# Top-k attention and a SwiGLU block on one core: the first nine units handled straight through, FFN block 0 by halves, rounding steps set between single top-k operations, and a new order of exponentials, sums and normalization within a unit

## The chip, the core and the metric

The kernel runs on one core of one Trainium2 chip. The core has five engines, each with its own instruction queue, worked through in order: TensorE (PE; its weight loads are shown apart as PEld), VectorE (DVE), ScalarE (ACT), GpSimd (POOL) and SyncE (SP), which here issues all transfers between HBM and the on-chip memory SBUF. Matmul results land in PSUM, a second on-chip memory, from which ScalarE copies them. The metric is the device time in microseconds (us).

## What is computed

```python
# q, k, v: (8, 8, 576, 64) float32; the three weights are float64
scores = scale * np.matmul(q, k.transpose(0, 1, 3, 2))
kth = np.partition(scores, -32, axis=-1)[..., -32:-31]
scores = np.where(scores >= kth, scores, -1e9)
attn = np.exp(scores - scores.max(-1, keepdims=True))
attn = attn / (attn.sum(-1, keepdims=True) + 1e-09)
o = np.matmul(attn, v)
x = o.transpose(0, 2, 1, 3).reshape(4608, 512)
g = x @ w_gate                                   # (512, 1536)
out = (g * (1 / (1 + np.exp(-g))) * (x @ w_val)) @ w_out   # (1536, 512)
```

Only the 32 largest of the 576 scores of each query count. The attention output of all heads is one token matrix `x`, on which the gated feed-forward block (FFN) works.

## The kernel before

**Units.** Attention is cut into 160 units, in the order batch (8), query tile (5), head pair (4): `units`, line 219. Four query tiles have 128 queries, so a unit holds two heads of 128 x 576 scores; the fifth has 64 queries, and its unit holds both heads on 128 partitions at once, half the work ("half units", units 16 to 19 of each batch of 20).

**A unit's steps.** `prep` (once per head pair and batch) transposes k and q on TensorE and ScalarE copies them to `kqT`. `scores` makes four PSUM banks `s`, which ScalarE copies to `sc`. `select` finds the 32 largest on VectorE: per head four MAX8 with three MATCH_REPLACE8 between them, and then one operation that sets `e` to a large negative number where a score is below the 32nd. `penalize` adds `sc` to `e` on POOL. `weigh` takes the exponential on ScalarE, with the row sum `tot`. `normalize` adds 1e-9 and takes the reciprocal of `tot` on VectorE, then ScalarE multiplies `e` by it. `turn` transposes `e` on TensorE, nine 128 x 128 tiles through three PSUM tiles `etps` (of four, one and four), and ScalarE copies them to `et`. `values` multiplies with v into `av`, and ScalarE copies that to the token block `xT`.

**PSUM.** The tiles `kqps`, `s`, `etps` and `av` share one pool of five buffers, given out in turn; `f` and `o_ps` of the FFN share three.

**FFN.** 4608 tokens make 18 blocks of 256. `feed` gives out a block in 36 pieces: 24 of four matmuls `f` (half a product of gate or value), then 12 of two matmuls `o_ps`. When a product is complete, a closure for ScalarE is put on `on_act` (gate: tanh, scale, add one; value: a copy), and one for POOL's multiplication on `on_pool`; `flush` records them. A block can start when its 256 tokens are there for all four head pairs (line 482). Pieces are paid with `credit`: 4.6 per pass of the loop (2.3 for a half unit), at most 8 saved.

**Rounding.** The weights are float64. `rounded` (line 92) turns a piece of 128 x 256 into fp32 from its two 32-bit halves, `low` and `high`: a transfer `w`, two operations on POOL, two on ScalarE and three on VectorE, 72 pieces in all. `weights` runs the pieces as a pipeline: one `rounding` step records the transfer of piece n, the first operations of piece n-3, the bit operations of n-4 and the last of n-5. `need` runs further steps when the FFN reaches a weight that isn't ready.

**The order.** The program text is the order: lines 576 to 590 chain the instructions of each compute engine in the order in which they are recorded. Pass n of the main loop (line 523) records, in this order: the penalty of unit n-1, the normalization of n-2, the values of n-3, the scores of n+1, and then the eleven or so steps of the top-k of n, with rounding steps, FFN pieces, the transposes of n-2 and the exponentials of n-1 between them. The VectorE part of `normalize(n-1)` stands between top-k steps.

## Time and profile before

| | |
|---|---|
| median of 3 runs | 1973.16 us (1972.95 to 1974.05) |
| the profiled execution | 1975.04 us, of which the span of its instructions is 1973.2 us |
| TensorE busy | 1779.5 us, 90% of the span |
| VectorE busy | 1640.1 us, 83% |
| ScalarE busy | 1156.0 us, 59% |
| POOL busy | 773.0 us, 39% |
| mean granted TensorE clock | 0.942 of full speed |

In a wait line, "A <- B: t, n, l" says that engine and line A stood idle until B for t us in all, n times, at most l us. In a timeline line the columns are start (us), duration (us), engine, line, operation, output<-inputs, shape, and the number of instructions taken together. One matmul of the program is two records in the trace, except for transposes, which are one. A line number with L is a line of the kernel. Matmul ends are modelled, so the next start is the better measure.

### The profile page before, as it was taken

The page shows a single profiled execution, that of the slowest core. Times are in us where ns is not written, and L with a number is a line of the kernel's source. Part 1 is how long each engine was busy: PE and PEld are TensorE (multiplying, and loading weights), DVE is VectorE, ACT ScalarE, POOL GpSimd, SP SyncE. Part 2 cuts the span into 40 slices and gives each one's busy share as a digit, 9 for nine tenths or more (in the row PEclk, how much of TensorE's full clock was granted, in tenths as well). Part 3 has the DMA queues.
Part 4 walks back from the last instruction along what each step waited for, and adds up shares of the span by engine and source line. Part 5 has one row for each costly group of instructions (what it writes and reads, how often), then busy time and mean ns, then how long its engine had stood idle before and what let it go on. Part 6 is the DMA issues. An engine that isn't in the chain of part 4 may idle for free.

```text
span 1973.2 us, 29487 instructions
## 1 busy us (share of the span) xinstructions
PE 1779.5 (90%) x10144; PEld 1297.7 (66%) x10144; DVE 1640.1 (83%) x3708; ACT 1156.0 (59%) x2821; POOL 773.0 (39%) x686
## 2 busy tenths in 40 slices
PE   3444779989999999999999999989999999899899
PEld 1223655847686867686768686858686867586666
DVE  5999687998889998989799898998898988889700
ACT  3555455656575656666667566656675656565512
POOL 2555453424334434343434352434343434243412
PEclk6566789999999999999999999999999999999999
DMA  5222111100030002100030002000120002000000
GB/s 153 84 80 75 43 50 43 44 12 1 9 79 11 1 12 57 30 1 11 4 78 7 12 2 68 18 11 1 33 54 11 1 14 50 11 1 11 1 11 11
DMA packets 111253, 59.58 MB, mean 30 GB/s; under 512 B 89088, under 2 KB 97280, under 8 KB 111104
## 3 DMA queue, kind: packets, MB, share of 16 engines
q1 hardware_dynamic: 111104, 57.70, 11.1%
q8 instruction: 80, 1.31, 0.3%
q14 instruction: 69, 0.57, 0.1%
HBM read 48.23 MB, written 9.44 MB: 29 GB/s over the span
## 4 chain that ended last, share of the span: by engine, by line
PE 78%; DVE 13%; issue 3%; ACT 3%; POOL 2%; SPq 1%; DMA 1%; POOLq 0%; ACTq 0%; DVEq 0%
PE f L418 37%; PE o_ps L452 18%; PE av L364 7%; PE etps L335 6%; PE s L256 6%; DVE m L277 5%; DVE rest L281 4%; PE s L242 2%; PE av L355 1%; PE kqps L211 1%; DVE bits L117 1%; DVE e L287 1%; DVE bits L114 1%; ACT e L308 1%; POOL bits L121 1%
## 5 line engine op out<-in xcount | busy, mean ns | idle before, releaser
L299 POOL TENSOR_TENSOR e<-e,sc 128x1152 f32<-128x1152 f32 (+1 forms) x160 | 383.0, 2394 | 731.3 <-DVE e L287 487.1
L277 DVE MAX8 m<-rest 128x8 f32<-128x576 f32 x864 | 613.7, 747 | 2.2
L418 PE MATMUL f<-xT,wg 128*128 128x256 f32 x1728 | 423.1, 391 | 16.7 <-ACT xT L379 16.7
L281 DVE MATCH_REPLACE8 rest<-m,rest 128x576 f32<-128x576 f32 x576 | 423.9, 743 | 0.0
L418 PE MATMUL f<-xT,wv 128*128 128x256 f32 x1728 | 409.3, 384 | 0.0
L452 PE MATMUL o_ps<-wo,h 128*128 128x512 f32 x864 | 400.1, 599 | 4.4 <-DVE wo L124 4.4
L418 PEld LDWEIGHTS f<-xT,wg 128*128 128x128 f32 x1728 | 323.4, 194 | 89.7 <-issue 27.8
L336 ACT COPY et<-etps 128x512 f32<-128x512 f32 (+1 forms) x448 | 195.1, 477 | 305.8 <-PE etps L335 305.2
L418 PEld LDWEIGHTS f<-xT,wv 128*128 128x128 f32 x1728 | 321.0, 193 | 48.3 <-issue 9.9
L335 PE MATMUL etps<-ident,e 128*128 128x128 f32 (+1 forms) x1312 | 207.4, 289 | 122.2 <-ACT sc L261 70.5
L335 PEld LDWEIGHTS etps<-ident,e 128*128 128x128 f32 (+1 forms) x1312 | 168.0, 148 | 202.8 <-issue 99.1
L323 ACT ACTIVATE e<-e,tot 128x576 f32<-128x576 f32 x288 | 209.5, 770 | 133.7 <-DVE tot L320 133.7
L452 PEld LDWEIGHTS o_ps<-wo,h 128*128 128x128 f32 x864 | 153.6, 190 | 163.6 <-issue 156.0
L439 POOL TENSOR_TENSOR h<-h,half_g 128x512 f32<-128x512 f32 x108 | 137.9, 1277 | 265.3 <-ACT h L438 258.8
L308 ACT ACTIVATE e<-e,bias 128x576 f32<-128x576 f32 x288 | 221.6, 776 | 4.1 <-POOL e L299 4.1
L277 DVE MAX8 m<-sc 128x8 f32<-128x576 f32 x288 | 205.1, 749 | 10.1 <-ACT sc L261 10.1
L281 DVE MATCH_REPLACE8 rest<-m,sc 128x576 f32<-128x576 f32 x288 | 212.0, 743 | 0.0
L256 PE MATMUL s<-kqT 64*128 64x288 f32 x1024 | 172.7, 459 | 11.4 <-ACT kqT L216 11.3
L364 PE MATMUL av<-et,v 128*64 128x128 f32 (+1 forms) x2560 | 178.5, 281 | 2.1 <-ACT et L336 1.0
L261 ACT COPY sc<-s 128x288 f32<-128x288 f32 x512 | 167.2, 416 | 12.8 <-PE s L256 12.3
L318 DVE TENSOR_SCALAR tot<-tot 128x2 f32<-128x2 f32 (+1 forms) x160 | 25.4, 159 | 168.0 <-ACT e L308 168.0
L444 POOL TENSOR_TENSOR h<-h,val 128x512 f32<-128x512 f32 x108 | 139.1, 1288 | 60.7 <-ACT val L443 60.3
(45 smaller groups left out, 1459.8 us busy)
## 6 DMA issues: line engine op xcount, KB each, us to landing
kq_in<-in_k_dram SPq DMA_DIRECT2D x64, 128.0 KB, 2.8
kq_in<-in_q_dram SPq DMA_DIRECT2D x64, 128.0 KB, 3.0
v<-in_v_dram SPq DMA_DIRECT2D x32, 256.0 KB, 3.0
w<-in_moe_w_gate_dram SPq DMA_DIRECT2D x24, 256.0 KB, 2.7
w<-in_moe_w_val_dram SPq DMA_DIRECT2D x24, 256.0 KB, 2.7
w<-in_moe_w_out_dram SPq DMA_DIRECT2D x24, 256.0 KB, 2.5
out_dram<-o SPq DMA_DIRECT2D x40, 128.0 KB, 2.4
out_dram<-o SPq DMA_DIRECT2D x16, 256.0 KB, 2.4
```

Source lines behind the costliest of these rows:

```text
L256: nc.tensor.matmul(ps[:, 0:half], slab[d, q0 : q0 + P], slab[d, k0 : k0 + half])
L261: nc.scalar.copy(sc[:, i * half : (i + 1) * half], ps[:, 0:half])
L277: nc.vector.max(m[:, t, 8 * r : 8 * r + 8], cur[:, hs])
L281: nc.vector.match_replace(rest[:, hs], m[:, t, 8 * r : 8 * r + 8], cur[:, hs], LOWEST)
L299: nc.gpsimd.tensor_tensor(e[:, every], e[:, every], sc[:, every], ALU.add)
L308: nc.scalar.activation(e[:, hs], e[:, hs], AF.Exp, bias=bias[:, t : t + 1], scale=scale, accum_out=tot[:, t : t + 1],)
L323: nc.scalar.mul(e[:, hs], e[:, hs], tot[:, t : t + 1])
L335: nc.tensor.transpose(ps[0:kl, c * P : (c + 1) * P], e[:, k0 : k0 + kl], ident[:])
L336: nc.scalar.copy(et[0:kl, c0 : c0 + cn, :], ps[0:kl, 0 : cn * P].rearrange("p (c j) -> p c j", c=cn),)
L364: nc.tensor.matmul(av[hh * R : (hh + 1) * R, 0:ql], v_last[:, hh, :] if c == J else vt[:, hh, c, :], moving, start=last and c == 0, stop=c ...
L418: nc.tensor.matmul(ps[:, i, :], w[:, c, m * P : (m + 1) * P], x[:, c, :], start=(c == 0), stop=(c == KC - 1),)
L452: nc.tensor.matmul(ps[:], hs[m // 2][:, m % 2, t * P : (t + 1) * P], wo[:, m, :], start=(m == 0), stop=(m == MC - 1),)
```

## The change

- **Rounding.** The absolute value is taken first (ScalarE), then clamped from below and above on POOL, then shifted; the sign and top bit now come from `high` itself. One VectorE operation of three is gone. Small values are no longer set to zero but clamped to the smallest size. `w` has 7 buffers instead of 4, `bits` 3, and the pipeline's last lag is 6 instead of 5.
- **Rounding steps** are no longer recorded in bunches but by a rate, 10/15 per top-k operation up to pass 4 and 6/15 after it. `select` yields after every single operation.
- **Head.** In passes 0 to 8 unit n-1 goes through all its steps (exponentials, sums, normalization, transposes, values) in pass n. q, k and v of the first batch's later pairs are loaded from within the passes.
- **Block 0** of the FFN runs in two halves of 128 tokens; the first can begin after unit 3 instead of unit 7. A head pass earns 8 credits; at most 10 are saved.
- **Order in a unit, in all passes.** ScalarE's FFN work is flushed and the exponentials of unit n-1 recorded right after the first FFN piece, ahead of the copies of the scores of n+1. After the head, the sum's VectorE operations stand at the end of the top-k.
- `sc` has 2 buffers instead of 3, `m` 2 instead of 3. At m = 6 of an output tile, pending ScalarE and POOL work is flushed.

```diff
@@ rounded @@
-        w = ffn.tile([P, n, 2], I32, tag="w", name="w", bufs=4)
+        w = ffn.tile([P, n, 2], I32, tag="w", name="w", bufs=7)
...
-        nc.gpsimd.tensor_scalar(
-            hi[:], high.bitcast(FP32), HUGE, -HUGE, ALU.min, ALU.max
-        )
+        size = conv.tile([P, n], FP32, tag="size", name="size")
+        nc.scalar.activation(size[:], high.bitcast(FP32), AF.Abs)
+        nc.gpsimd.tensor_scalar(size[:], size[:], HUGE, LEAST, ALU.min, ALU.max)
         ulps = conv.tile([P, n], I32, tag="ulps", name="ulps")
         nc.scalar.mul(ulps[:], low.bitcast(U32), 2.0**-29)
-        size = conv.tile([P, n], FP32, tag="size", name="size")
-        nc.scalar.activation(size[:], hi[:], AF.Abs)
         yield
...
         nc.vector.tensor_scalar(
-            bits[:], hi, 3, 0x3FFFFFFF, ALU.logical_shift_left, ALU.bitwise_and
-        )
-        nc.vector.scalar_tensor_tensor(
-            out=bits[:], in0=hi, scalar=-0x40000000, in1=bits[:],
-            op0=ALU.bitwise_and, op1=ALU.bitwise_or,
+            bits[:], size[:].bitcast(I32), 3, 0x3FFFFFFF,
+            ALU.logical_shift_left, ALU.bitwise_and,
         )
         nc.gpsimd.tensor_tensor(bits[:], bits[:], ulps[:], ALU.add)
         yield
         nc.vector.scalar_tensor_tensor(
-            out=dst, in0=size[:], scalar=LEAST, in1=bits[:].bitcast(FP32),
-            op0=ALU.is_ge, op1=ALU.mult,
+            out=dst.bitcast(I32), in0=high, scalar=-0x40000000, in1=bits[:],
+            op0=ALU.bitwise_and, op1=ALU.bitwise_or,
         )
@@ weights @@
-            for lag in (5, 4, 3, 0):
+        lags = (6, 4, 3, 0)
@@ scores, select @@
-        sc = work.tile([P, 2 * S], FP32, tag="sc", name="sc", bufs=3)
+        sc = work.tile([P, 2 * S], FP32, tag="sc", name="sc", bufs=2)
-        m = small.tile([P, 2, TOP_K], FP32, tag="m", name="m")
+        m = small.tile([P, 2, TOP_K], FP32, tag="m", name="m", bufs=2)
@@ feed @@
+        halves = [slice(0, P), slice(P, BLK)] if kb == 0 else [slice(0, BLK)]
+        for c in halves:
+            while done[kb] < NHP * c.stop:
+                yield 0
...
                 need(8 * MS + 2 * m + 2)
+                if m == 6:
+                    flush(on_act)
+                    flush(on_pool)
@@ before the loop @@
     load(0)
-    rounding(3)
+    rounding(4)
     load(1)
-    for i in range(NHP):
-        if i > 1:
-            load(i)
-        load_v(i)
@@ the loop @@
+    HEAD = 2 * NHP + 1
+    due = [0.0]
     for n in range(NU + 3):
+        head = n < HEAD
...
+        turned = turn(n - 2) if HEAD - 1 <= n - 2 < NU else no
+        rate = (10 if n < NHP + 1 else 6) / 15
+        def dve(k):
+            for _ in range(k * nh):
+                next(topk, None)
+                due[0] += rate
+                if due[0] >= 1:
+                    due[0] -= 1
+                    rounding(1)
         if n < NU:
-            credit[0] = min(credit[0] + (2.3 if units[n][1] == J else 4.6), 8.0)
+            new = 8.0 if head else 4.6 if nh == 2 else 2.3
+            credit[0] = min(credit[0] + new, 10.0)
         flush(on_act)
         if 0 <= n - 1 < NU:
             penalize(n - 1)
         run(over.pop(n - 2, no))
         flush(on_pool)
-        if n >= 3:
-            values(n - 3)
...
+        if n - 3 >= HEAD - 1:
+            finish_unit(n - 3)
         next(nxt, None)
-        next(topk, None)
-        next(topk, None)
-        rounding(1 + (n < 2 * NHP + 2))
+        dve(1)
+        if head:
+            if 2 <= n + 2 < NHP:
+                load(n + 2)
+            if 0 <= n - 1 < NHP:
+                load_v(n - 1)
+        dve(1)
         pieces(1)
+        flush(on_act)
+        if 0 <= n - 1 < NU:
+            weigh(n - 1)
         next(nxt, None)
+        flush(on_pool)
         next(turned, None)
-        flush(on_act)
         pieces(1)
         next(turned, None)
         flush(on_act)
-        if 0 <= n - 1 < NU:
-            weigh(n - 1)
-        flush(on_pool)
...
+        dve(2)
         next(ahead, None)
         pieces(1)
         next(ahead, None)
...
+        dve(1)
+        if head:
+            next(over[n - 1], None)
         pieces(1)
...
+        dve(1)
+        if head:
+            run(over.pop(n - 1))
+            pieces(1)
+            if n >= 1:
+                run(turn(n - 1))
+        dve(1)
+        if head:
+            pieces(1)
+            if n >= 1:
+                finish_unit(n - 1)
+        else:
+            next(over[n - 1], None)
+        run(topk)
+        if not head:
+            next(over[n - 1], None)
         pieces(6)
```

`finish_unit(n)` calls `values(n)` and, for the last query tile of a batch, loads v of the next batch.

## The prediction

> **What bounds the kernel now.** I read the windows by stage first, then TensorE's waits, then VectorE's, then the timeline of one loop pass. A pass n of the main loop runs the top-k of unit n, the scores of unit n+1, and later steps of earlier units.
>
> ```profile
> 0.00:50.00 50.00, 16.16 (x66) 10.22 (x68) 27.80 (x71) 19.39 (x52) 13.32 (x25) 0.69 0.60 155
> 50.00:200.00 150.00, 68.05 (x311) 45.25 (x310) 136.45 (x338) 76.75 (x204) 76.96 (x102) 0.60 0.26 78
> 200.00:330.00 130.00, 101.67 (x503) 71.72 (x503) 100.02 (x224) 67.79 (x169) 62.24 (x72) 0.84 0.12 38
> 330.00:450.00 120.00, 111.04 (x682) 82.40 (x680) 112.26 (x253) 76.81 (x193) 43.66 (x34) 0.94 0.14 37
> 450.00:1880.00 1430.00, 1393.76 (x8279) 1028.59 (x8280) 1263.59 (x2825) 897.64 (x2174) 559.08 (x439) 0.99 0.08 21
> ```
>
> Columns: stretch, length, busy time of PE, PEld, DVE, ACT, POOL, granted clock, DMA. Up to about 450 us TensorE idles (153 us in all, at a clock of 0.60 between 50 and 200) and VectorE carries the time. From 450 to 1880 TensorE is busy 97%. So a microsecond saved on VectorE counts in the head, and after 450 us only one saved or lost on TensorE counts.
>
> ```profile
> PE etps L335 <- ACT sc L261: 70.5, 13, 6.9
> ```
>
> ```profile
> DVE wo L124 <- POOL bits L121: 23.6, 6, 6.9
> DVE tot L318 <- ACT e L308: 14.6, 10, 4.7
> DVE bits L114 <- POOL hi L102: 12.4, 10, 9.8
> ```
>
> Microseconds, times, longest. The first line is TensorE's largest wait, over the whole span (all of it in the head): the transposes into `etps` wait for ScalarE to copy scores out of PSUM. The other three are VectorE's waits up to 450 us. Last, one pass in the steady part:
>
> ```profile
> 645.72 0.79 ACT L308 ACTIVATE e<-e,bias 128x576 f32<-128x576 f32 x1
> ...
> 646.48 0.78 ACT L308 ACTIVATE e<-e,bias 128x576 f32<-128x576 f32 x1
> ...
> 647.24 0.58 ACT L443 COPY val<-f 128x512 f32<-128x512 f32 x1
> ...
> 648.34 1.24 PE L256 MATMUL s<-kqT 64*128 64x288 f32 x8
> ...
> 649.51 1.99 PE L418 MATMUL f<-xT,wg 128*128 128x256 f32 x8
> ...
> 650.94 1.30 ACT L261 COPY sc<-s 128x288 f32<-128x288 f32 x4
> ...
> 651.34 0.71 PE L335 MATMUL etps<-ident,e 128*128 128x128 f32 x5
> ```
>
> TensorE goes from scores to one FFN piece to transposes without a gap; the score copies come right after the scores, and the exponentials later in the pass.
>
> **Part 1, the rounding, VectorE: -24 us.** A piece's three VectorE instructions start 0.32, 0.34 and 0.33 us apart (14.28, 14.60, 14.94; 38.29, 38.62), 0.99 us; two remain, 0.66. 72 x 0.33 = 24 us, all in the VectorE-bound head, so on the path. ScalarE keeps two operations a piece (0.33 each to the next start) and POOL two; only their order changes (|w| first, the clamp behind it).
>
> **Part 2, the head.** VectorE's own sum, up to the end of unit 28 (block 2 of the FFN needs unit 27): 27 whole-unit equivalents x 10.63 us (first MAX8 of two successive units at 651.15 and 661.78) = 287, start 11.5, rounding 71: 370. The trace has that end at 443.8, so 74 us of waiting and slowed operations; block 2 begins at 449.9.
> - Gone: `wo` on `bits` 23.6 (rounding ends by pass 9 instead of 16), most of `tot` 14.6 (the sums now follow the top-k) and 9.8 of the wait on `hi` (SyncE issued 28 transfers of q, k, v, 10.3 to 28.7 us, ahead of that weight; they are now spread over passes 0 to 4). Each SyncE issue costs about 0.6 us (0.59 to 0.64); per early pass some 9 weight transfers and up to 10 loads, 11 us of a pass of 18, so SyncE hides them. With that cover gone the 9.8 returns.
> - New, start: four rounding steps are recorded before unit 0's preparation, so ScalarE's |w| of piece 0 stands ahead of the first `kqT` copy (5.59). It needs the weight landed near 8.2: +1.5 us.
> - New, POOL: 9.3 rounding steps per unit instead of 5 meet POOL's penalty addition (2.64 us) at each unit's start. The nearest rows are one `bits` of 2.72 us instead of 0.42 and one of 1.36 instead of 0.29. 9 units x 1.3 = 12 us; bounds 0 and 9 x 2.3 = 21.
> - New, first half block (passes 4, 5): unit 3's reciprocal comes after 12 of 14 top-k steps of pass 4 (15 us), normalization takes 1.44, transposes and av at half clock 2.15 and 2.9, copies the rest: 23 us, 5 into pass 5. Then 7 products of 8 matmuls stand ahead. Two records each of 128 columns, 0.11 (transposes, 5 in 0.55) to 0.155 (`vlast`, 2 in 0.31), taken 0.13: 15 us, plus 4 for the first ones at half clock. ScalarE has the gates of these products in its queue ahead of the next |w| steps, the exponentials of unit 4 and the score copies of unit 6. VectorE, in order, stands at the first blocked rounding step some 4 us into pass 5: 5 + 15 + 4 - 4 = 20 us lost; bounds 13 (0.11, no half clock) and 26. Block 0's halves cost TensorE at most 384 x (0.155 - 0.11) = 17 us more, beside its idle time.
> - New, second half (passes 8 to 11): the same, with 12 products and the scores of units 10 and 11 queued behind them: 20 us; bounds 10 and 28.
> - New, pass 18: ten pieces at once (17 us) ahead of the next scores, while VectorE has two half units left: 8 us; bounds 0 and 15.
>
> Of the 74, the first item takes away 45 (12 of `tot`), and 18 (`wg`, `wv` waits and slowed operations) are the same collisions that the POOL term now counts; 11 stay. Waits then: 12 + 20 + 20 + 8 + 11 = 71, bounds 30 and 90 (passes 10 to 17, now bare of rounding, may take some back). Unit 28 ends at 370 + 1.5 - 24 + 71 = 418.5, and block 2 starts about 10 us later instead of 6 (unit 27's reciprocal now comes after unit 28's last operation): 428.5 against 449.9. **Head: -21 us, between -62 and -2.**
>
> **Part 3, the order within a unit, in the steady part: the term that decides.** `weigh` is moved ahead of the score copies, and a flush of ScalarE's pending FFN work ahead of `weigh`. In the changed program's order ScalarE does: normalization of unit n-2, `xT` copy, [value copy, gate or output copy, if the pass's first FFN piece ended one], two exponentials, four score copies. Behind the first score copy waits TensorE: the fifth transpose of a pass takes the PSUM buffer of the first score bank (5 buffers; allocations per pass: av, four banks, three etps). That is the pair in the 70.5 us row, so it can stop TensorE.
>
> Passes whose first piece ends nothing: the exponentials run while TensorE is still on av and scores, provided VectorE is ahead. VectorE needs 10.63 us a unit, TensorE about 12.2 (649.51 to 661.75), so it is: 0 us. It was not ahead before (unit end at 651.2, after the scores) because it waited 153 us for exponentials after 460 us. That wait goes and gains nothing, VectorE being 88% busy beside a full TensorE. Without that lead each such pass would stop some 4 us.
>
> Passes whose first piece ends a product: with the piece's start as 0, the fifth transpose is due at 2.27 (651.34 - 649.51 + 4 x 0.11). The value copy starts at 2.06 (0.07 after the piece's end, as at 647.24), the next operation 0.49 later, the exponentials take 1.52 (645.72 to 647.24), the copy 0.42: 4.49, and 0.07 more until TensorE starts. TensorE stands 2.3 us; behind it are the rest of the transposes, all further pieces and the next scores. A gate (three operations, 1.46) gives 3.3, an output copy 2.4. From block 2 on, with full score banks: 19 value passes with two exponentials x 2.3, 3 with one x 1.5, 8 outputs x 2.4, 5 gates (13.2 + 2.5): **+83 us**, bounds 35 x 0.5 = 18 (the nearest small wait of TensorE on ScalarE, av on `et`, 2.4 us in 5) and 35 x 3.9 = 137 (the stop at 218.97 in the head, where ScalarE's queue was blocked in the same way). I take 83, built from durations of the very instructions.
>
> Absorbed: TensorE waits 32.7 us between 460 and 1880, where FFN work runs out. VectorE's new lead takes part of it, but the first transposes after such a gap now wait for exponentials too: -10, between -25 and 0.
>
> Fewer buffers for `sc` and `m` cost 0: the score copy already stands behind the exponentials that free them. The credit cap and the flush at m = 6 move a few pieces by a pass: 0, covered by TensorE's full queue.
>
> **Two rules of the Trainium skill.** The slowed `bits` rows come when POOL adds. "SBUF — State Buffer", section "SBUF: two separate sides", says VectorE and GpSimd share a port pair as an exclusive lock, the loser blocking for the whole instruction. By it each collision could cost up to the full 2.64, so the POOL term 9 x 2.64 = 24 instead of 12. And: after 3.21 us without work two output records took 2.07 us, where four take 1.88. "TensorE: Matmul & The Clock Gate" (Part 1) puts the fall to half clock at about 3.4 us of idleness; by it only the gate stops (3.3) come near, and a few microseconds each would be added.
>
> **Sum.** The profiled execution took 1975.04 us with a span of 1973.2; the median of the runs is 1973.16, 1.9 below that execution, so span changes are added to the median: 1973.2 - 21 + 83 - 10 = 2025. **Forecast 2025 us, slower.**
>
> **Rivals.**
> - *The stop is not there* (ends faster): ScalarE is through with the value copy and exponentials before the fifth transpose is due. For it: ScalarE is 63% busy, and TensorE's gap-free passes show some slack. Against: the copy cannot start before the piece ends. Head -21, stop 15, absorbed -20: 1947. It decides once the stops sum to less than the 31 us of head gain and absorption, 0.9 us for each of 35 passes.
> - *The head gains nothing or loses*: both half-block bursts and POOL at their upper bounds. For it: ScalarE's in-order queue; against: passes 10 to 17 run without rounding. 1973 - 2 + 90 - 5 = 2056.
> - *Head gain and stops cancel* (head -60, stops 75, absorbed -16): 1972.
>
> **Chances.** Forecast 0.64 (own range 1990 to 2050), faster rival 0.20 (1925 to 1965), worse head 0.12, cancelling 0.04. Range 1940 to 2060. About 0.2% (4 us) is what a measurement of this kernel can tell from no change: faster 0.21, same 0.03, slower 0.76.
>
> **What would show it.** Right: TensorE's waits gain a row of `etps` on the score copies or the value copy of 60 to 100 us after 450 us, 2 to 3.5 us each; VectorE's wait of `tot` on exponentials nearly vanishes; block 2 starts near 428. The first half block shows VectorE waiting some 20 us in one place near 100 us. Wrong: no such row, TensorE still 97% busy after block 2; then the head decides and the kernel is faster. Also wrong: VectorE not getting ahead, which makes the row larger than 110.

## The result and the profile after

The changed kernel took 2072.18 us (median of 4 runs, 2071.54 to 2080.4) against 1973.61 us for the kernel before beside it: 1.0509 times as long, 95% interval 1.0482 to 1.0535. The profiled execution took 2071.54 us with a span of 2069.7. The forecast was 2025 us, slower, in 1940 to 2060: the sign was right, the size was 47 us short and outside the range.

The stretches that the prediction read, in the profile of the changed kernel (stretch, length, busy time of PE, PEld, DVE, ACT, POOL, granted clock, DMA):

```profile
0.00:50.00 50.00, 16.38 (x71) 10.94 (x71) 35.62 (x85) 28.13 (x74) 25.13 (x44) 0.71 0.68 185
50.00:200.00 150.00, 65.86 (x472) 57.23 (x472) 119.95 (x280) 86.86 (x228) 88.98 (x130) 0.70 0.32 98
200.00:330.00 130.00, 110.39 (x703) 79.87 (x701) 102.41 (x230) 72.24 (x182) 48.63 (x48) 0.91 0.05 14
330.00:450.00 120.00, 99.50 (x546) 69.02 (x545) 111.00 (x249) 68.57 (x175) 35.58 (x25) 0.87 0.10 26
450.00:1880.00 1430.00, 1329.70 (x7664) 968.38 (x7663) 1184.45 (x2633) 827.09 (x2017) 526.87 (x411) 0.98 0.08 20
```

TensorE was busy 97% of the last stretch before; now it is 93%, and VectorE falls from 88% to 83%. Both engines do the same work over a longer stretch.

The best cut is the start of block 2 of the FFN: 449.9 us before, 440.8 after, so the head gained 9 us. From there to the end it was 1523.3 us and is 1628.9, so 106 us are lost in the steady part. TensorE's waits in that second stretch of the changed kernel:

```profile
PE etps L329 <- ACT sc L255: 88.6, 58, 3.1
PE av L349 <- ACT et L330: 7.9, 10, 1.7
PE f L413 <- ACT xT L373: 4.5, 3, 1.8
PE av L358 <- ACT et L330: 2.5, 4, 1.2
```

and, as the largest, in that of the kernel before:

```profile
PE f L418 <- ACT xT L379: 14.9, 6, 4.4
```

The first row of the changed kernel did not exist there before: 58 waits of the fifth transpose for a score copy. One such pass:

```profile
486.43 1.24 PE L250 MATMUL s<-kqT 64*128 64x288 f32 x8
...
487.60 1.99 PE L413 MATMUL f<-xT,wv 128*128 128x256 f32 x8
...
489.43 0.60 PE L329 MATMUL etps<-ident,e 128*128 128x128 f32 x4
...
489.69 0.59 ACT L446 COPY val<-f 128x512 f32<-128x512 f32 x1 [2.87 <-PE f L413]
...
490.17 0.78 ACT L302 ACTIVATE e<-e,bias 128x576 f32<-128x576 f32 x1
...
490.94 0.76 ACT L302 ACTIVATE e<-e,bias 128x576 f32<-128x576 f32 x1
...
491.70 1.29 ACT L255 COPY sc<-s 128x288 f32<-128x288 f32 x4
...
492.13 0.33 PE L329 MATMUL etps<-ident,e 128*128 128x128 f32 x1 [2.10 <-ACT sc L255]
```

The scores were ready at about 487.6, but ScalarE stood idle for 2.87 us in front of the value copy, which waits for a piece that TensorE had just begun. The exponentials and the score copies stood behind it, and TensorE came round to the same queue 2.10 us too early.

In the head, VectorE's waits up to 450 us are now:

```profile
DVE bits L110 <- POOL size L103: 46.7, 33, 12.5
DVE tot L312 <- ACT e L302: 21.0, 5, 12.0
DVE m L271 <- ACT sc L255: 11.5, 2, 11.2
```

The wait of `wo` on the addition (23.6) is gone, as forecast; a wait for the clamp (46.7) stands in its place, and `tot` grew from 14.6 to 21.0.

### The profile page after: what moved, and what is told of

The parts are those of the page before. It is cut to its first block, busy times and chain, and to the rows that moved or that the text cites. A ratio compares the mean times of both kernels' runs of the same rounds, so it can differ in the third digit from the quotient of the medians.

```text
span 2069.7 us, 29856 instructions
## 1 busy us (share of the span) xinstructions
PE 1802.5 (87%) x10336; PEld 1312.0 (63%) x10336; DVE 1626.7 (79%) x3636; ACT 1156.7 (56%) x2845; POOL 776.3 (38%) x698
## 4 chain that ended last, share of the span: by engine, by line
PE 72%; ACT 11%; DVE 11%; POOL 3%; issue 2%; DMA 0%; SPq 0%; ACTq 0%; POOLq 0%
PE f L413 35%; PE o_ps L459 18%; PE av L358 6%; PE etps L329 6%; PE s L250 5%; ACT e L302 5%; DVE m L271 4%; DVE rest L275 4%; PE s L236 2%; POOL e L293 1%; ACT e L317 1%; ACT sc L255 1%; PE av L349 1%; PE kqps L205 1%; POOL bits L114 1%
## 5 line engine op out<-in xcount | busy, mean ns | idle before, releaser
L413 PE MATMUL f<-xT,wg 128*128 128x256 f32 (+1 forms) x1824 | 419.6, 379 | 4.5 <-ACT xT L373 4.5
L413 PE MATMUL f<-xT,wv 128*128 128x256 f32 (+1 forms) x1824 | 416.1, 376 | 0.0
L459 PE MATMUL o_ps<-wo,h 128*128 128x512 f32 x864 | 407.9, 609 | 0.0
L329 PE MATMUL etps<-ident,e 128*128 128x128 f32 (+1 forms) x1312 | 218.5, 291 | 210.9 <-ACT sc L255 105.9
L413 PEld LDWEIGHTS f<-xT,wg 128*128 128x128 f32 x1824 | 331.1, 195 | 60.1 <-issue 15.3
L413 PEld LDWEIGHTS f<-xT,wv 128*128 128x128 f32 x1824 | 328.3, 194 | 59.6 <-issue 22.2
L441 POOL TENSOR_TENSOR h<-h,half_g 128x512 f32<-128x512 f32 (+1 forms) x114 | 139.5, 1223 | 365.0 <-ACT h L440 347.9
L312 DVE TENSOR_SCALAR tot<-tot 128x2 f32<-128x2 f32 (+1 forms) x160 | 27.3, 170 | 279.8 <-ACT e L302 279.6
L447 POOL TENSOR_TENSOR h<-h,val 128x512 f32<-128x512 f32 (+1 forms) x114 | 138.8, 1217 | 185.1 <-ACT val L446 184.5
L250 PE MATMUL s<-kqT 64*128 64x288 f32 x1024 | 167.1, 447 | 9.3 <-ACT kqT L210 9.0
L438 ACT ACTIVATE h<-f 128x512 f32<-128x512 f32 (+1 forms) x114 | 65.7, 576 | 181.5 <-PE f L413 181.5
```

Of the source, the lines that this page charges most:

```text
L250: nc.tensor.matmul(ps[:, 0:half], slab[d, q0 : q0 + P], slab[d, k0 : k0 + half])
L329: nc.tensor.transpose(ps[0:kl, c * P : (c + 1) * P], e[:, k0 : k0 + kl], ident[:])
L413: nc.tensor.matmul(ps[:, i, 0:n], w[:, kc, m * P : (m + 1) * P], x[:, kc, c], start=(kc == 0), stop=(kc == KC - 1),)
L441: on_pool.append(lambda: nc.gpsimd.tensor_mul(hc, hc, gc))
L459: nc.tensor.matmul(ps[:], hs[m // 2][:, m % 2, t * P : (t + 1) * P], wo[:, m, :], start=(m == 0), stop=(m == MC - 1),)
```

## Experiments: what makes the steady part slower

My theory was that the order of a pass on ScalarE alone costs the 106 us. Its rivals were a cause in the head or in the place of the sums. Four kernels were run side by side first.

**Order of a pass as before** (changed kernel, `weigh` and the flushes moved back):

```diff
         pieces(1)
-        flush(on_act)
-        if 0 <= n - 1 < NU:
-            weigh(n - 1)
         next(nxt, None)
-        flush(on_pool)
         next(turned, None)
+        flush(on_act)
         pieces(1)
         next(turned, None)
         flush(on_act)
+        if 0 <= n - 1 < NU:
+            weigh(n - 1)
+        flush(on_pool)
```

> The changed kernel with only the order of a pass put back as it was: piece, score products, transposes, held copies, piece, score copies with the fifth transpose, held copies, exponentials, held product. My theory: the new order alone makes the 58 stops of the fifth transpose (88.6 us after the second block began), their half-clock stretches (some 24 us) and their drains (some 11 us), and took 18 us of TensorE's other waits away. So the stops go, the stretch from the second block to the end comes back from 1629 to about 1523 us, and the time is about 1960 to 1970 us, some 9 us under the kernel before, since the head's gain stays. Rival: the rounding or the whole of the head has shifted the steady part as well, and then the time stays above 2030 us with the stops there in part.

Measured: 1976.54 us (ratio to the kernel before 1.0011, 1.0002 to 1.002). The wait of `etps` on score copies after the second block fell to 5.9 us. So the order of a pass carries about 96 us of the loss. The time is 6 us over the upper end of what I expected: the stretch after block 2 took 1537.6 us, 14 more than in the kernel before. Half clock held there for 46.0 us, against 25.4 in the kernel before. If work takes twice as long in it (1.88 and 3.49 us in the rows of the fill run below), half of the difference, about 10 us, is in the 14. Block 2 began at 437.6 us, 3 earlier than in the changed kernel.

**Only the held copies moved back**, exponentials still early:

```diff
         pieces(1)
-        flush(on_act)
         if 0 <= n - 1 < NU:
             weigh(n - 1)
         next(nxt, None)
+        next(turned, None)
+        flush(on_act)
         flush(on_pool)
-        next(turned, None)
         pieces(1)
         next(turned, None)
```

The held copies now stand behind the fifth transpose's copy, ahead of the last four transposes.

> The changed kernel with the exponentials still ahead of the score copies, but the held FFN copies and products moved behind the score copies and the last transposes. My theory: what makes the stop is the held value, gate or output copy, which stands on ScalarE ahead of the score copies and waits for the FFN piece that TensorE has just begun; so the stops of 2 to 3 us go, the waits of some 0.2 us may stay, and the time is 1955 to 1985 us. Rival: the two exponentials (together about 2.5 us of ScalarE) hold up the score copies by themselves, and then the stops stay at 1 to 2 us each and the time stays above 2030 us.

Measured: 1952.41 us (0.989, 0.9876 to 0.9905), now faster than the kernel before and 3 us under the lower end of my range. Two waits and a pass of this run:

```profile
PE etps L329 <- ACT sc L255: 14.1, 25, 2.2
PE av L349 <- ACT et L330: 4.5, 10, 0.6
```

```profile
477.97 1.24 PE L250 MATMUL s<-kqT 64*128 64x288 f32 x8
...
478.25 0.78 ACT L302 ACTIVATE e<-e,bias 128x576 f32<-128x576 f32 x1
...
479.02 0.76 ACT L302 ACTIVATE e<-e,bias 128x576 f32<-128x576 f32 x1
...
479.14 1.99 PE L413 MATMUL f<-xT,wv 128*128 128x256 f32 x8
...
479.78 1.29 ACT L255 COPY sc<-s 128x288 f32<-128x288 f32 x4
...
480.97 0.71 PE L329 MATMUL etps<-ident,e 128*128 128x128 f32 x5
...
482.25 0.60 ACT L446 COPY val<-f 128x512 f32<-128x512 f32 x1
```

This pass too ends a value product in its first piece. The exponentials now run while TensorE does the scores, the score copies while it does the piece, and five transposes go without a gap. After block 2 the early exponentials are harmless; the early flush is the fault.

**The same order on the kernel before** (its sums, rounding and head untouched):

```diff
         pieces(1)
+        flush(on_act)
+        if 0 <= n - 1 < NU:
+            weigh(n - 1)
         next(nxt, None)
+        flush(on_pool)
         next(turned, None)
-        flush(on_act)
         pieces(1)
         next(turned, None)
         flush(on_act)
-        if 0 <= n - 1 < NU:
-            weigh(n - 1)
-        flush(on_pool)
```

> The kernel before with only the new order of a pass (held copies and exponentials ahead of the score copies, held product ahead of the last transposes); sums, rounding and head as before. My theory: the stops come with the order alone, so the fifth transpose stops some 58 times for about 89 us after the second block began, and the time is 2060 to 2085 us, a little over the changed kernel, which has the shorter head. Rival: the new place of the normalization and sums, or the head, makes the stops; then this order costs under 40 us and the time is under 2015 us.

Measured: 2110.3 us (1.0678, 1.0656 to 1.0701), with this row after the second block:

```profile
PE etps L335 <- ACT sc L261: 99.3, 48, 3.1
```

The order alone is enough, as expected. It costs 136 us there, 25 more than the upper end of my expectation: 22 of the 34 stops over 1.5 us took about 3.05 us, the length of a gate's stop, where the changed kernel has 4 such stops; half clock held for 100.9 us after block 2, a cost that a later run measures; and block 2 began 15 us later.

**What a stop is made of.** Held copies early, exponentials late:

```diff
         flush(on_act)
-        if 0 <= n - 1 < NU:
-            weigh(n - 1)
         next(nxt, None)
...
         flush(on_act)
+        if 0 <= n - 1 < NU:
+            weigh(n - 1)
```

> The changed kernel with the held copies still ahead of the score copies, but the exponentials behind the last transposes again. My sum for a stop was: piece, held copy, two exponentials, score copy; without the exponentials' 1.52 us a stop after a value is 2.1 - 1.5 = 0.6 us, after a gate 1.5, after an output 0.5. So the stops sum to 20 to 30 us instead of 88, hardly any half clock follows, and the time is 1985 to 2010 us. Rival: the held copy alone makes the stop whatever stands behind it, and it stays near 2 us each and above 2040 us; or it is harmless alone, and the time is that of the run with before's order, 1973 to 1980 us.

Measured: 2009.98 us (1.0182, 1.0167 to 1.0197). The row and two of its stops, after a value and after an output:

```profile
PE etps L329 <- ACT sc L255: 29.8, 44, 1.5
```

```profile
491.80 0.33 PE L329 MATMUL etps<-ident,e 128*128 128x128 f32 x1 [0.59 <-ACT sc L255]
...
620.15 0.33 PE L329 MATMUL etps<-ident,e 128*128 128x128 f32 x1 [0.54 <-ACT sc L255]
```

Behind gates it stands 1.54 us. All three are what was expected (0.6, 0.5 and 1.5): the stop is the plain sum of piece, held copy, exponentials and score copy, minus the time until the fifth transpose is due. The half clock is not what was expected: it held for 48.9 us after block 2. Most of these stretches follow other waits of TensorE, of 1.8 to 3.3 us (for `xT` or `kqT`, or ahead of transposes).

**What a stop costs beside its own length.** The changed kernel, with the four first transposes repeated in the 45 passes whose first piece ended a product; the repeats write the same values again:

```diff
+            if c0 == 0 and held[0]:
+                for c in range(4 * cn):
+                    k0 = (c % cn) * P
+                    nc.tensor.transpose(
+                        ps[:, (c % cn) * P : (c % cn + 1) * P], e[:, k0 : k0 + P], ident[:]
+                    )
...
         pieces(1)
+        held[0] = n >= 28 and bool(on_act)
         flush(on_act)
```

> The changed kernel with TensorE kept at work during the stops: in passes from 28 on whose first piece ended a product, the four first transposes are repeated four more times (16 records of 0.11 us, 1.8 us) ahead of the fifth, so a stop of 2.1 us shrinks to some 0.3 us and the same time passes with work that changes nothing. Theory that the stops also cost half clock after them (82 us at half clock after the second block, 29 us in the run without stops): the half-clock time falls to 35 to 50 us and the time falls by 15 to 25 us, to 2045 to 2057 us. Rival: the half clock has another cause, or the stops are the whole loss; then the half-clock time stays and the time stays within 6 us or grows: 2066 to 2085 us.

Measured: 2064.4 us (1.046, 1.0443 to 1.0478), 8 us under the changed kernel, between the two expectations. The row of the stops here:

```profile
PE etps L330 <- ACT sc L256: 30.1, 57, 2.2
```

The same place in both kernels, the changed one first (TensorE's timeline), then this run:

```profile
504.96 0.33 PE L329 MATMUL etps<-ident,e 128*128 128x128 f32 x1 [2.10 <-ACT sc L255]
505.13 3.49 PE L459 MATMUL o_ps<-wo,h 128*128 128x512 f32 x4
```

```profile
502.92 1.91 PE L334 MATMUL etps<-ident,e 128*128 128x128 f32 x16
505.18 0.33 PE L330 MATMUL etps<-ident,e 128*128 128x128 f32 x1 [0.35 <-ACT sc L256]
505.35 1.88 PE L466 MATMUL o_ps<-wo,h 128*128 128x512 f32 x4
```

The four records behind the stop took 3.49 us, and 1.88 behind the filled one. The windows of the changed kernel give the clock of that stretch, 0.55:

```profile
504.90:508.40 3.50, 3.44 (x5) 1.28 (x6) 3.50 (x9) 1.56 (x6) 2.56 (x1) 0.55 0.02 5
```

The stretch after block 2 as a whole, the changed kernel first, then this run:

```profile
440.80:2069.70 1628.90, 1517.70 (x8590) 1100.88 (x8588) 1266.93 (x2814) 908.06 (x2206) 580.57 (x453) 0.98 0.08 19
441.00:2062.30 1621.30, 1571.72 (x9310) 1165.49 (x9308) 1267.46 (x2814) 908.18 (x2206) 580.08 (x453) 0.99 0.08 19
```

Summed over it by the trace's records of the granted clock, half clock held for 72.9 us in the changed kernel and 20.8 us with the fill, better than the theory of half clock expected. (By the same records the expectation's 82 us are 72.9, and the run without stops, the one with the held copies late, has 16.2.) The time fell by less than expected because I had forgotten the price of the fill in passes that hardly stopped. The bill: 45 x 16 records x 0.11 = +79 us of work; the `etps` row 88.6 to 30.1, -58.5; other waits -3; half clock (72.9 - 20.8) / 2 = -26. That is -8.5, and the stretch went from 1628.9 to 1621.3, -7.6. So half clock behind the stops cost about 26 us on top of their own length.

## Experiments: what happened in the head

**The new rounding alone**, on the kernel before:

```diff
-        hi = conv.tile([P, n], FP32, tag="hi", name="hi")
-        nc.gpsimd.tensor_scalar(
-            hi[:], high.bitcast(FP32), HUGE, -HUGE, ALU.min, ALU.max
-        )
+        size = conv.tile([P, n], FP32, tag="size", name="size")
+        nc.scalar.activation(size[:], high.bitcast(FP32), AF.Abs)
+        nc.gpsimd.tensor_scalar(size[:], size[:], HUGE, LEAST, ALU.min, ALU.max)
...
-        nc.vector.scalar_tensor_tensor(
-            out=bits[:], in0=hi, scalar=-0x40000000, in1=bits[:],
-            op0=ALU.bitwise_and, op1=ALU.bitwise_or,
-        )
...
-            out=dst, in0=size[:], scalar=LEAST, in1=bits[:].bitcast(FP32),
-            op0=ALU.is_ge, op1=ALU.mult,
+            out=dst.bitcast(I32), in0=high, scalar=-0x40000000, in1=bits[:],
+            op0=ALU.bitwise_and, op1=ALU.bitwise_or,
```

> The kernel before with only the new rounding (two VectorE operations for each piece in place of three, the clamp by magnitude ahead on ScalarE and GpSimd); lags, pace and head as before, with five buffers of raw pieces, since seven don't fit beside three of the scores. My theory: VectorE sets the pace of the head and gets back 0.33 us for each of 72 pieces, 24 us at most, and the steady part is untouched: 1950 to 1965 us. Rival: the chain of magnitude, clamp, shift and addition across ScalarE and GpSimd sets the pace in place of VectorE, and the time is within 5 us of the kernel before.

Measured: 1920.98 us (0.9731, 0.9716 to 0.9745), 53 us, twice the most that I expected. Block 2 starts at 394.1 instead of 449.9, and the steady part is unchanged (1523.6). VectorE's groups of the kernel before in the first 450 us (count, busy us, mean ns, idle before):

```profile
L117 DVE SCALAR_TENSOR_TENSOR bits<-hi,bits 128x256 int32<-128x256 int32 x72 | 33.8, 470 | 2.5
...
L114 DVE TENSOR_SCALAR bits<-hi 128x256 int32<-128x256 int32 x72 | 23.8, 331 | 12.4 <-POOL hi L102 12.4
...
L124 DVE SCALAR_TENSOR_TENSOR wo<-size,bits 128x256 f32<-128x256 f32 x24 | 11.0, 459 | 23.6 <-POOL bits L121 23.6
```

and of the new rounding alone:

```profile
L110 DVE TENSOR_SCALAR bits<-size 128x256 int32<-128x256 int32 x72 | 24.9, 346 | 14.0 <-POOL size L103 14.0
...
L117 DVE SCALAR_TENSOR_TENSOR wo<-w,bits 128x256 int32<-128x256 int32 x24 | 11.0, 460 | 1.4 <-POOL bits L114 1.4
```

Two things went. Added up from each start to the next, waits left out, all rounding operations together held VectorE for 81 us before and 46 us after, 0.49 us for each of 72 pieces and not 0.33: the operation that is left out had taken 0.40 us in the mean, and the shift now takes 0.09 less. And `wo`'s wait for the addition, 23.6 us, fell to 1.4, although pace and lags were as before; why, no run shows. 35 + 22 make the 56 us.

So the rest of the head's rearrangement cost 47 us. The following runs split it.

**Exponentials early, held copies late, on top of the rounding:**

```diff
         pieces(1)
+        if 0 <= n - 1 < NU:
+            weigh(n - 1)
         next(nxt, None)
         next(turned, None)
         flush(on_act)
         pieces(1)
         next(turned, None)
         flush(on_act)
-        if 0 <= n - 1 < NU:
-            weigh(n - 1)
         flush(on_pool)
```

> The kernel before with the new rounding, and with the exponentials ahead of the score copies but the held FFN copies and products behind them (the order that stopped little on top of the changed kernel). Sums, pace of the rounding and head as before. My theory: the exponentials ahead are harmless and even worth some 5 us after the second block, since the stretch from the second block to the end was 1518 us with them and 1524 us without; the head stays that of the new rounding alone (second block at 394 us). So 1910 to 1918 us, the fastest of all. Rival: the 5 us came from the normalization first, or from the sums last, which are not in here; then 1918 to 1930 us, with more small stops and no gain.

Measured: 1924.35 us (0.9749, 0.9735 to 0.9764). The time is the rival's, but not for its reason: the steady part took 1514.6 us, 9 less than before, so the early exponentials do gain there; the head lost 13.5 (block 2 at 407.6). VectorE's first wait in that head shows what came back:

```profile
DVE wo L117 <- POOL bits L114: 18.4, 6, 5.7
```

**Block 0 whole** (on the run with the held copies late, as are all that follow but the last):

```diff
-        halves = [slice(0, P), slice(P, BLK)] if kb == 0 else [slice(0, BLK)]
+        halves = [slice(0, BLK)]
...
-                if not todo or done.get(todo[0], 0) < NHP * (BLK if todo[0] else P):
+                if not todo or done.get(todo[0], 0) < NHP * BLK:
```

> The run with the held copies late (1952.4 us), with block 0 of the FFN in one piece of 256 tokens, begun after unit 7 as in the kernel before. Where the head loses its gain: the theory that the half blocks' bursts do it gives back the 14 and 6 us of passes 5 and 6 and the 14 us of pass 9, less what the same work costs later: second block 10 to 25 us earlier than 433 us, 1927 to 1942 us. The theory that the rounding's chain of single steps does it gives at most 8 us here: 1944 to 1960 us.

Measured: 1937.63 us (0.9815, 0.9801 to 0.983), 15 us less; block 2 at 416.3 instead of 432.7. The half blocks lose 16 us of the head, in passes 5 and 6 (28.2 and 20.5 us with halves, 16.6 and 15.3 without; a pass is counted from the first MAX8 of its unit to that of the next). VectorE's wait on the clamp falls from 46.2 to 27.7 us. Pass 9, where the second half begins, stays long: 26.4 us with halves, 27.1 without.

**One more step of lag:**

```diff
-        lags = (6, 4, 3, 0)
+        lags = (7, 5, 3, 0)
```

with 8 buffers of `w`, 3 of `size` and `ulps`, 2 of `bits` instead of 3, and one of the output tile.

> The run with the held copies late (1952.4 us), with one more rounding step between magnitude and shift and one more between the addition and the last operation (8 buffers of raw pieces, 3 of magnitude; 1 buffer of the output tile instead of 2 to make room). Theory of the chain: VectorE's wait of the shift on the clamp (46 us in 35 times in the head) falls under 10 us and the second block begins 25 to 35 us earlier, 1918 to 1930 us. Theory of the half blocks' bursts: the steps are blocked because ScalarE is blocked, so another step of lead only moves the wait, and the gain is under 10 us: 1942 to 1955 us.

Measured: 1946.89 us (0.9862, 0.9846 to 0.9879), 5.5 us less. VectorE's waits up to 425 us:

```profile
DVE tot L312 <- ACT e L302: 13.7, 2, 12.9
DVE m L271 <- ACT sc L255: 11.8, 2, 11.5
DVE wv L117 <- POOL bits L114: 11.1, 1, 11.1
DVE wo L117 <- POOL bits L114: 10.0, 2, 9.0
...
DVE bits L110 <- POOL size L103: 0.6, 2, 0.3
```

The wait of the shift on the clamp fell from 46 to 0.6 us as the chain theory said, and yet the time hardly moved. 21 us came back in three waits on the addition, and the rounding's own operations grew from 54 to 71 us (the last one from 0.55 to 0.69 us a piece). Here a wait that was removed inside the chain came back at its next link; the two `bits` buffers may have a part in that, which no run tells apart.

**No straight run:**

```diff
-    HEAD = 2 * NHP + 1
+    HEAD = 0
```

with the first loads ahead of the loop again.

> The run with the held copies late (1952.4 us), without the straight-through head: the first nine units are pipelined over passes as all others, and the first batch is loaded ahead of the loop as in the kernel before; rounding's pace and half blocks stay. If running a unit straight through in the next pass is what costs the head (sums waiting for exponentials 13 us, ScalarE's queue in front of the magnitudes), the second block begins 15 to 30 us earlier and the time is 1922 to 1938 us. If the pace of the rounding is what costs, the early passes still take about 20 us each and the time stays within 8 us: 1944 to 1962 us.

Measured: 1950.96 us (0.9882, 0.9868 to 0.9897); block 2 at 431.3 instead of 432.7. With half blocks, running a unit straight through costs nothing to speak of.

**No rounding in the first quarter of a pass:**

```diff
-                if due[0] >= 1:
+                if due[0] >= 1 and not hold:
...
-        dve(1)
+        dve(1, True)
```

(both `dve(1)` ahead of the first piece)

> The run with the held copies late (1952.4 us), with no rounding step in the first quarter of a pass (the first four top-k operations), where GpSimd does the penalty's addition of 2.6 us; the steps held back are made up one by one after it. Theory of contention with GpSimd: in the new pace rounding falls into that addition, so that VectorE either waits for the clamp behind it (46 us in the head) or runs its two-input operation slowed (0.55 us each instead of 0.36); with the steps behind the addition both go down, the two-input operation to 0.40 us or less, the wait under 25 us, and the time is 1920 to 1937 us. Rival: the single steps are too close to each other wherever they stand, and the wait and the slowing only move to the rest of the pass: 1945 to 1958 us.

Measured: 1968.58 us (0.9967, 0.9956 to 0.9979), 16 us more. Both expectations were wrong. Why it is slower is not shown.

**The rounding steps back in their old places**, with half blocks and with block 0 whole:

```diff
-                due[0] += rate
-                if due[0] >= 1:
-                    due[0] -= 1
-                    rounding(1)
...
+        rounding(1 + (n < 2 * NHP + 2))
         pieces(1)
```

and `rounding(1)` behind three later top-k steps.

> The run with the held copies late (1952.4 us), with the rounding steps put back where they were in the kernel before: five a pass in four places up to pass 9, four a pass after it, each behind two top-k steps. If the new pace is what the head loses (waits of the shift on the clamp 46 us, the last operation at 0.55 us instead of 0.36), these fall to about 14 us and 0.36 us and the second block begins 15 to 25 us earlier: 1927 to 1938 us. If the loss is in the half blocks and the straight run alone, 1946 to 1956 us.

> The run with block 0 whole (1937.6 us), with the rounding steps put back as well. If pace and half blocks are two separate losses that add up, the second block begins at 394 to 402 us as with the new rounding alone, and the time is 1912 to 1924 us. If they overlap, so that either one hides the other, 1930 to 1938 us.

Measured: 1957.84 us with half blocks (0.992, 0.9903 to 0.9936) and 1936.38 us with block 0 whole (0.9808, 0.9794 to 0.9823): 5 us more and 1 us less than with the new pace. So the pace is not the loss here, and the losses do not add up in the way I expected. The first of the two shows what the faster pace is for. Early passes took 14.5 us instead of 20, but the first half block then began at 88 us and found no weights:

```profile
PE etps L329 <- POOL bits L114: 53.9, 6, 13.6
PE f L413 <- DVE wg L117: 12.6, 8, 3.5
...
PE f L413 <- DVE wv L117: 9.2, 8, 3.1
```

and pass 5 took 64 us, with 24 pieces of rounding in it where its neighbours have 5 or 6.

**Slower rate of single steps:**

```diff
-        rate = (10 if n < NHP + 1 else 6) / 15
+        rate = 6 / 15
```

> The run with the held copies late, with 6 rounding steps to 15 top-k operations from the start instead of 10 up to pass 4; the steps still stand singly. If the rate is too high for the chain over ScalarE and GpSimd, the early passes fall from 20 to 17 us and part of it stays: 1930 to 1945 us. If single steps cost the same at any rate, 1947 to 1957 us.

Measured: 1963.07 us (0.9948, 0.9933 to 0.9963), 11 us more. Early passes took 16 us, and pass 5 took 59: the same thing. Neither expectation had it.

**Neither straight run nor half blocks**, new pace:

```diff
-    HEAD = 2 * NHP + 1
+    HEAD = 0
...
+        halves = [slice(0, BLK)]
```

with the first loads ahead of the loop.

> The run with the held copies late, without the straight-through head and with block 0 whole, so that of the head's changes only the rounding itself, its pace and its buffers remain. If the pace costs some 20 us by itself, 1930 to 1942 us. If it costs only where units run straight through, 1915 to 1926 us.

Measured: 1940.98 us (0.9836, 0.9822 to 0.9851); block 2 at 421.9. Against the early exponentials on the kernel before (407.6), what is left of the change in the head (pace, buffers, sums last) costs 14 us. Within the straight head the old places of the steps gained nothing, so the price of the pace depends on what stands around it.

**A version that beats both.** New rounding on the kernel before, its order up to pass 27, from pass 28 on exponentials early and held copies late:

```diff
         pieces(1)
+        early = n >= 28
+        if early and n - 1 < NU:
+            weigh(n - 1)
         next(nxt, None)
...
-        if 0 <= n - 1 < NU:
+        if not early and n >= 1:
             weigh(n - 1)
```

> The kernel before with the new rounding, in the order of before up to pass 27 and with the exponentials ahead of the score copies (held copies behind them) from pass 28 on. The two runs it is put together from had the second block at 394 us (order of before) and a stretch from there to the end of 1515 us (exponentials ahead). If the two add up, 1909 to 1915 us, faster than both kernels and than every run so far. Rival: the short steady stretch of the one run came from its later head (work piled up), and then 1916 to 1922 us.

Measured: 1912.07 us (0.969, 0.9676 to 0.9705), 63 us under the kernel before and 160 under the changed one. The steady part took 1514.0 us.

The runs make a ladder from one kernel to the other (starts of block 2 and the rest of the span from the profiles, us):

| kernel | block 2 starts | from there on | median |
|---|---|---|---|
| before | 449.9 | 1523.3 | 1974 |
| + new rounding | 394.1 | 1523.6 | 1921.0 |
| + exponentials early | 407.6 | 1514.6 | 1924.4 |
| + straight head, buffers, sums last, the rest | 416.1 | 1518.4 | 1936.4 |
| + single rounding steps | 416.3 | 1520.9 | 1937.6 |
| + half blocks | 432.7 | 1518.1 | 1952.4 |
| + held copies early = changed kernel | 440.8 | 1628.9 | 2072.2 |

The steps depend on their order, as the run without straight head shows, and the first run of all: on the changed kernel the old order of a pass brings block 2 forward by 3 us only, where the ladder's two steps of order cost 13.5 and 8. The two ends do not depend on it.

## Why the prediction was right and wrong

- **The stop: right, its size with some luck.** The chain of copies and the PSUM bank were named, 83 us were forecast, 88.6 were found; 2.10, 3.05 and 2.05 us a stop instead of 2.3, 3.3 and 2.4. The sum of a stop holds in two more kernels (late exponentials, and the order on the kernel before). The 35 stops that the prediction counted are there by kind and number, but come to 75 us; 23 others make up the rest, 16 of them of 0.2 us. It takes the early flush, as the prediction's passes without a held copy said: with the exponentials alone the row is 14.1.
- **The step that failed: nothing was put down for what a stop does to the work behind it.** Some 24 us of half clock against the kernel before ((72.9 - 25.4) / 2) were left out; the fill run puts it at 26. The prediction knew the row (two records in 2.07 us after a wait of 3.21) and gave it no term. In the trace after, half clock set in during or within 2.6 us behind 17 of the 36 stops longer than 1.5 us. Sixteen of these were 1.9 to 2.2 us long, and one was a gate's of 3.05, the only one of four. In the run with late exponentials it followed 4 of 44, waits under 0.8 us that have other waits close by, and none of its five of 1.5 us. The Trainium skill's page "TensorE: Matmul & The Clock Gate", Part 1, lets the clock fall after about 3.4 us without work, by which only the gates' stops came near. The traces do not agree with that, and the measurement decides: here 2.1 us were enough, though not each time.
- **Also at nothing: the transposes around a stop, 11 us.** The last transpose before a stop lasted 0.27 us by its record and the one behind it 0.18 to the next start, where one in flow takes 0.11: 0.23 us for each of 58 stops, 13 us, which the row of waits does not hold. Of the 106 us, 11 are left without them (106 - 88.6 - 24 + 17.6).
- **Absorbed: -10, found -17.6.** TensorE's other waits after block 2 fell from 35.1 to 17.5 us.
- **Part 1, rounding: -24 forecast, mis-sized.** One spacing of 0.33 us, read from one place, was taken for all 72 pieces; the new rounding alone gives 0.49. The wait of `wo` that I credited to rounding's earlier end went with the new rounding itself. In the changed kernel the rounding operations took 54 us instead of 81, which is 27 less, with 14 us of slowing by GpSimd in it.
- **Part 2, the head: -21 forecast, -9 found.** Unit 28 ended at 429.9 us, forecast 418.5. Start and own work of VectorE came to 348 us against 347.5, waits and slowed operations to 82 against 71. Term by term: GpSimd 14 (forecast 12), first half block 20 in passes 5 and 6 (20), second 14 in pass 9 (20), the wait that I take for that of the ten pieces at once 12 in pass 19 (8), the rest 22 (11). Of the 14 in pass 9, 12 stand also with block 0 whole. The step that failed here is that rest. It was put at what stayed of the old waits, but the new pace brought waits of its own: 26 of the shift on the clamp in passes 0 to 4 and 8, 21 of them of 0.29 us, 12.6 us in all; `tot` added 9 us in passes 22 to 25. By the ladder the order of a pass, priced only after block 2, takes 22 us of the head; put back on the changed kernel it gives 3, so that price hangs on the rest.
- **GpSimd's term has its rows.** The last operation of a piece took 0.55 us instead of 0.36 (14 us in 72). One that met the penalty's addition, and that addition:

```profile
72.03 2.62 POOL L293 TENSOR_TENSOR e<-e,sc 128x1152 f32<-128x1152 f32 x1
...
72.58 2.36 DVE L117 SCALAR_TENSOR_TENSOR wg<-w,bits 128x256 int32<-128x256 int32 x1
```

  Six met it; they took 1.58 to 2.47 us, and each ended 0.28 to 0.29 us after the addition. The Trainium skill's page "SBUF — State Buffer", section "SBUF: two separate sides", says that the two engines block each other there for a whole instruction; the trace agrees. The prediction's 24 us by that page took nine collisions over a whole addition; six happened, begun 0.4 to 1.4 us into it.
- **The lead of VectorE: the sign of its row was wrong.** The wait of `tot` on exponentials did not vanish; it went from 168 to 279.6 us over the span. VectorE is ahead and waits there, while TensorE sets the time.
- **The rivals.** "Head gains nothing" came nearest (2056), with the wrong account. "The stop is not there" is the run with late held copies (1952.4 against its 1947), whose condition, ScalarE through before the fifth transpose is due, the flush broke.

Of the 47 us, 44.5 are in the span: head 12, stops 5.5, half clock 24, transposes at the stops 11, less 8 more absorbed. The rest is the difference between the profiled executions and the medians.

## What to carry to other kernels

On an engine that works in order, a copy that waits for the newest work of a second engine should not stand ahead of one that gives the second engine its next buffer. Put the ready work first: here the place of one flush was worth 120 us. Price a stop of TensorE with what the clock takes from the work behind it, which here was about 30% more. And when a change has several parts, price the gain of each alone: here one part was worth 53 us alone, and the rest hid it.

## What the hardware showed that was not expected

- Half clock after stops of only 1.9 to 2.2 us, mostly 3.4 us long, at nearly half of the stops over 1.5 us; filling the stop with transposes that change nothing took the half-clock time from 72.9 to 20.8 us.
- The new rounding, with one two-input operation of VectorE less, saved more than a spacing in a quiet place: 0.49 us instead of 0.33 a piece, and with it a wait of 22 us on GpSimd's addition.
- An operation of VectorE with two inputs that met GpSimd's addition ended 0.28 to 0.29 us after it in all six cases, up to 2.47 us long instead of about 0.4.
